# Block 1's q in an attention + SwiGLU kernel: half of its transfers issued by ScalarE, its two turns placed around block 0's last product of h, and block 0's sums behind them

## The chip, the core and the metric

The kernel runs on one core of a Trainium2 chip. TensorE (PE; its weight loads are shown apart as PEld) multiplies, VectorE (DVE), ScalarE (ACT) and GpSimd (POOL) work on tiles, SyncE (SP) only issues DMAs, and ACT can issue them too. Each engine runs its own instruction list strictly in order and meets the others through semaphores. The metric is the device time of one launch in microseconds (us), as the median of several runs.

## What is computed

Inputs are float32. Attention is linear (no softmax): for each of 8 batches and 8 heads a 64x64 matrix is made from k and v, q is multiplied by it, and each row of 64 is divided by its root mean square. The result, laid out as 4608 tokens by 512, goes through a SwiGLU block with 1536 hidden columns.

```
kv  = einsum('bhsd,bhse->bhde', k, v)          # 8 batches, 8 heads, 576 positions, 64 wide
o   = einsum('bhsd,bhde->bhse', q, kv)
o   = o / sqrt(mean(o * o, -1) + 1e-6) * g_norm
x   = o.transpose(0, 2, 1, 3).reshape(4608, 512)
g, val = x @ w_gate, x @ w_val                 # 512 x 1536 each
out = (g * sigmoid(g) * val) @ w_out           # 1536 x 512
```

## The kernel before

The 4608 tokens are nine blocks of 512. For each block an `Att` object makes x (attention, turned so that features lie on partitions) and an `Ffn` object makes h = silu(x w_gate) * (x w_val) and then h w_out. Blocks 0, 1 and 2 run alone, the other six in pairs. Most of the feed-forward multiplications use Strassen's scheme in Winograd's form: seven products (numbered 1 to 7) take the place of eight, and VectorE and GpSimd make the sums and differences of operands and results that it needs. The time of interest is the end of block 0 and the start of block 1, some 98 to 160 us into the launch.

**Block 0, up.** Block 0's h is made without Strassen, in `plain_up(f)` for f = 0 to 11: eight matmuls into one `b` and one `c` bank of PSUM (L1475), ScalarE's silu of `b` into h (L1480), VectorE's product of h with `c` (the helper `mul`, L133). Beside it the weights are loaded by SP (L177) and rounded by VectorE and ScalarE (L188 to L204); the last of them go into `wo`. Then `t2` takes a difference and a sum in `wo` (helpers `sub`, L132, and `add`, L131).

**Block 1's inputs.** When the last weight pieces are under way, SP issues block 1's k and v (L317, 288 KB each) and its q (L338): two halves of 16 small DMAs each, 8 of 56 KB and 8 of 8 KB, all with runs of 32 floats, into two tiles of the pool `ld`. `turn_q(0)` and `turn_q(1)` transpose the two halves on VectorE (L391) into one tile `qt`. A half of q here is a half of the heads, so each of block 1's products `heads` (L436) needs both.

**Block 0, down.** `plain_end` makes the sums of h: s1 = a21 + a22 (L131, 128x1536) and, over a21 in place, s1 - a11 (L132, 128x1536). Then `Ffn.down` issues the seven products of the down multiplication (`Quad.multiply`, L663) in the order 1, 6, 5, 7, 2, 4, 3 as traced, into the banks `b` (1, 6, 7, 4), `c` (5, 3) and `a` (2). Product 1 takes a11 alone, product 6 the new a21, product 5 takes s1. Each product is 24 matmul records. What follows them:

- after product 1, block 1's `heads` for both halves (L436), then on ScalarE their squares (L449), on VectorE four row sums (L450), an inverse root by nine 128x32 steps (L466 to L481), four scalings (L133) and two transposes (L515), then 16 DMAs (L527, 8 from SP and 8 from ACT) that put the turned blocks into x, ScalarE's gain (L534) and four sums of x on VectorE;
- `turn_s3`: one more difference in h (L132, 128x1536);
- after product 2 (`after2`): r = a + s (L131), then s4, a difference in h that product 3 multiplies (L132, 128x1536);
- after product 7 (`after7`): ScalarE copies `b` (L1376), and VectorE adds `c`, which holds product 5, to that copy (L131). Product 3 goes on into the same `c`, so it cannot start before this add has read the bank;
- `t2` on the six tiles `wv[j]` (for each a `sub` and an `add` of 128x512): j = 0 to 2 behind block 1's scaling, j = 3 to 5 behind s4. Block 1's weights need them, GpSimd's own differences `t` (L132 on POOL) among them.

**kept_steps.** Six steps for each half of a pair of weight tiles: three differences and a sum on VectorE (128x256 to 128x512), and two DMAs that send them to DRAM (L1259). They are handed to `ffn.later` in `Up.multiply` and taken by `make`.

**What sets the order.** The language traces instructions and a scheduler at compile time decides the order in which each engine gets them, by dependencies and by its own estimate of times. `tc.issue_after(i)` says that what is traced inside it and runs on i's engine comes behind i on that engine; it makes no wait between engines. `in_order` keeps the traced order on the engines named. So an edit can move instructions that its lines do not name.

Of the kernel before, what the change touches and what calls it, by code (L numbers as in the profile page):

```python
# [8 lines left out]
F32 = mybir.dt.float32  # L9
# [3 lines left out]
ACT = mybir.ActivationFunctionType  # L13

P = 128
# [3 lines left out]
def kernel(  # L19
# [41 lines left out]
    nc = tc.nc  # L61

    B, H, S, D = q.shape
    NT, DM = out.shape
    FF = moe_w_gate.shape[1]
    T = 4
    BLK = P * T
    HB = BLK // 2
    HD = DM // 2
    NB = NT // BLK  # L70
    NS = DM // P
    NF = FF // P
    NP = NF // 2
# [12 lines left out]
    s_pool = pool("s", 1)  # L86
# [148 lines left out]
    class Att:  # L235
# [305 lines left out]
        def sum_steps(self):  # L541

            a11, a12, a21, _, s1, s3, s4 = (self.x[:, i] for i in range(7))
            yield lambda: add(nc.vector, s1, a21, self.x[:, 3])
            yield lambda: sub(nc.vector, s3, a21, a11)
            yield lambda: sub(nc.vector, a21, s1, a11)
            yield lambda: sub(nc.vector, s4, a12, a21)
# [137 lines left out]
    class Up(Quad):  # L685
# [29 lines left out]
        def after7(self):  # L715
            self.u3 = self.piece(2)
            copied = nc.scalar.copy(out=self.u3, in_=self.ps["b"])

            if self.j < NP - 1:
                with tc.issue_after(copied.ins):  # L720
                    nc.scalar.activation(out=self.s, in_=self.s, func=ACT.Silu)
            added = add(nc.vector, self.u3, self.ps["c"], self.u3)

            owed, self.ffn.owed = self.ffn.owed, None
            if owed:
                with tc.issue_after(added.ins):
                    owed()
# [18 lines left out]
        def multiply(self, p):  # L746
            super().multiply(p)
            ffn = self.ffn
            if ffn.n == 1:
                if p == 5:  # L750
                    self.leaf_room = chunks(ring())
                if p in (5, 7, 4):
                    at = 3 * (5, 7, 4).index(p)
                    ffn.making.extend(leaf_steps(self.j, [(self.w[p].unsqueeze(1), (p,))], self.leaf_room[:, at:]))
                if p == 3:
                    if self.j < 2:
                        ffn.later.extend(kept_steps(self.j, chunks(xi_alone)))

    class Inner:

# [531 lines left out]
    def chunks(t):  # L1292

        return t.rearrange("p f (s c) -> p (f s) c", c=P) if len(t.shape) == 3 else t.rearrange("p a b c -> p (a b) c")

    def kept_steps(j, room):


        for i, (t, os) in enumerate(kept(j)):
            b11, b12, b22 = t[:, :, 0, 0], t[:, :, 0, 1], t[:, :, 1, 1]  # L1300
            to = room[:, 8 * i : 8 * (i + 1)].rearrange("p (o r) c -> p o r c", r=4)
            t2_ = to[:, :, 0]
            yield lambda b22=b22, b12=b12, t2_=t2_: sub(nc.vector, t2_, b22, b12)
            yield lambda b11=b11, t2_=t2_: add(nc.vector, t2_, t2_, b11)
            yield lambda t=t, t2_=t2_, to=to: sub(
                nc.vector, to[:, :, 2:4], t[:, :, 1], t2_.unsqueeze(2).to_broadcast([P, 2, 2, P])
            )
            yield lambda t2_=t2_, os=os: send_leaf(j, os, (6,), t2_)
            yield lambda b11=b11, t2_=t2_, to=to: sub(nc.vector, to[:, :, 1], b11, t2_)
            yield lambda to=to, os=os: send_leaf(  # L1310
                j, os, (7, 4, 5), to[:, :, 1:4].rearrange("p o r c -> p o (r c)")
            )
        if j < 2:
            yield from raw_steps(j)
# [72 lines left out]
    class Ffn:  # L1387
        def __init__(self, n, att):
            self.n, self.att = n, att
            self.h = h_alone if n < PAIRED else h_slots[(n - PAIRED) % 2]  # L1390
            self.ps, self.ended, self.owed = {}, None, None

            self.making, self.later = [], []
            self.chores, self.sends = [], []
            self.visited = None
# [5 lines left out]
        def h_sums(self, j, k, engine):  # L1401

            h = self.h.rearrange("p (j e) t -> p j e t", e=2)[:, j : j + k]
            a11, a21, a22 = h[:, :, 0, 0:HB], h[:, :, 0, HB:BLK], h[:, :, 1, HB:BLK]
            s1 = self.s1[:, j : j + k]
            add(engine, s1, a21, a22)
            return sub(engine, a21, s1, a11)

        def make(self, count):
            for _ in range(count):  # L1410
# [55 lines left out]
        def plain_up(self, f, halves=(0, 1)):  # L1466

            if 0 in halves:
                self.ps[f] = [pool.tile([P, 2, HB], F32, name=pool.name[0]) for pool in (b_psum, c_psum)]
            of = slice(halves[0], halves[-1] + 1)  # L1470
            ps = [t[:, of] for t in self.ps[f]]
            x = self.att.x[:, 0:4].rearrange("p (h m) i t -> p (m i) h t", h=2)
            for t, w in zip(ps, (wg, wv)):
                for i in range(NS):
                    nc.tensor.matmul(  # L1475
                        t, lhsT=w[f // 2][:, i, P * (f % 2) : P * (f % 2 + 1)], rhs=x[:, i, of],
                        start=(i == 0), stop=(i == NS - 1),
                    )
            h = self.h[:, f].rearrange("p (h t) -> p h t", h=2)[:, of]
            nc.scalar.activation(out=h, in_=ps[0], func=ACT.Silu)  # L1480
            mul(nc.vector, h, h, ps[1])

        def plain_end(self):

            self.s1 = s_pool.tile([P, NP, HB], F32, name="s1")
            self.h_sums(0, NP, nc.vector)
            self.down_ = Down(self)
            self.down_.turn_t(5)

# [72 lines left out]
    def t2(place, b22, b11):  # L1562

        sub(nc.vector, place, b22, place)
        add(nc.vector, place, place, b11)

    blocks = [Att(n) for n in range(NB)]
    blocks[0].room = h_alone
# [55 lines left out]
    def alone(n):  # L1624
        ffn = Ffn(n, blocks[n])
        nxt = blocks[n + 1]
        if n == 0:

            with tc.issue_after(squared.ins), tc.issue_after(scaled.ins):
                weights(2)  # L1630
            ffn.plain_up(0, (0,))
            copied = blocks[0].copied
            blocks[0].turn_x(1)
            for f in range(NF):
                with tc.issue_after(blocks[0].copied.ins if f else copied.ins):
                    weights(2 * (f + 2))
                ffn.plain_up(f) if f else ffn.plain_up(0, (1,))
            weights(len(pieces))
            pairs = wo.rearrange("p (j e) d -> p e j d", e=2)
            t2(pairs[:, 0, :, HD:DM], pairs[:, 1, :, HD:DM], pairs[:, 0, :, 0:HD])  # L1640
            nxt.room = xi_alone.rearrange("p a b c -> p (a b c)")

            with tc.issue_after(sent.ins):
                for i in range(2):
                    nxt.load_kv(i)
                for i in range(2):
                    nxt.load_q(i)
            ffn.plain_end()
            for g in range(2):
                nxt.kv(g)  # L1650
            nxt.turn()
        elif n == 1:

            def third():
                visit(ffn, nxt, (0, 1))
                for i in range(2):
                    nxt.load_q(i)

            ffn.up({(1, 7): third})
            nxt.turn()  # L1660
            blocks[PAIRED].load_kv(0)
        else:
            with in_order(nc.vector.engine, nc.scalar.engine):
                ffn.up(ahead(ffn, nxt, blocks[PAIRED + 1]))
            nxt = blocks[PAIRED + 1]
            nxt.turn()
            for g in range(2):
                blocks[PAIRED + 2].load_kv(g)
        if n == 2:
            ffn.down_.opens = PAIRED  # L1670

        def inner_sums():
            with tc.issue_after(nxt.scaled.ins):
                blocks[PAIRED].inner_sums()

        def second_kv():
            with tc.issue_after(nxt.placed.ins):
                blocks[PAIRED].load_kv(1)

        ffn.down(nxt, {1: {5: second_kv}, 2: {7: inner_sums}}.get(n, {}))  # L1680
        if n == 0:
            for g in range(2):
                blocks[2].load_kv(g)

            with tc.issue_after(nxt.halves[0].ins):
                for j in range(NP // 2):
                    t2(wv[j][:, 0:2], wv[j][:, 2:4], wg[j][:, 0:2])
            with tc.issue_after(ffn.down_.s4.ins):
                for j in range(NP // 2, NP):
                    t2(wv[j][:, 0:2], wv[j][:, 2:4], wg[j][:, 0:2])  # L1690

    for n in range(PAIRED):
        with in_order(nc.tensor.engine) if n == 2 else ExitStack():
            alone(n)
# [65 lines left out]
```

## Time and profile before

| What | Value |
|---|---|
| median of 3 runs | 1005.79 us (1004.57 to 1006.64) |
| the profiled execution's own time | 1004.97 us |
| its span from first to last instruction | 1003.2 us |
| granted TensorE clock over the span | 1.0 |
| instructions | 17762 |
| idle of PE over the span, 1003.2 - 986.9 | 16.3 us |
| HBM traffic | 109.12 MB read, 32.83 MB written |

A timeline row of the profile gives the start in us from the span's start, the time to the last end, the engine, the line, the operation, out<-in with the number of partitions and elements, and how many instructions were merged; in brackets stands the idle time before them and what ended it. An engine name with a q (SPq, ACTq, DVEq) is that engine's queue, which issues DMAs and waits. In the lists of waits a row says who waited for whom, with the sum, the number of times and the longest in us. Two of the steps above in numbers: SP's 32 issues of q took from 98.98 to 118.50 us, and the DMA engines were busy 0.40 of the time between 104.0 and 113.8 us, when only q was moving.

### The profile page before, as it was taken

How to read it: one execution, taken by the hardware profiler on the slowest of the kernel's cores; microseconds unless marked ns; L12 is line 12 of the kernel's file. 1: busy time of each engine (PE TensorE's matmuls, PEld its weight loads, DVE VectorE, ACT ScalarE, POOL GpSimd, SP SyncE). 2: the span in 40 equal slices, each digit the busy share in tenths (PEclk: the TensorE clock that was granted, in tenths of full speed). 3: DMA queues.
4: the chain of work that ended last, by engine and by line, in shares of the span. 5: the costliest groups of instructions: out<-in, count | busy, mean ns of one | idle time of the engine just before them, and what ended most of it. 6: DMA issues, size and time to landing. Idle time of an engine off the chain costs nothing.

```text
span 1003.2 us, 17762 instructions
## 1 busy us (share of the span) xinstructions
PE 986.9 (98%) x6758; PEld 833.6 (83%) x6758; DVE 713.1 (71%) x1171; ACT 231.5 (23%) x367; POOL 408.1 (41%) x328
## 2 busy tenths in 40 slices
PE   5999999999999999999999999999999999999998
PEld 4544688888888888888888888888888888888998
DVE  2999797579958576656675846666776576666894
ACT  2765111221122312121211211122112112222100
POOL 0000263255544240444566003555651078999300
PEclk9999999999999999999999999999999999999999
DMA  8689643473866855666752365667312556565123
GB/s 228 199 261 268 123 87 137 102 271 107 210 135 132 205 114 167 178 193 168 171 151 43 97 158 151 158 180 177 112 18 68 118 169 204 182 213 161 48 83 97
DMA packets 268261, 151.54 MB, mean 151 GB/s; under 512 B 150288, under 2 KB 250128, under 8 KB 268176
## 3 DMA queue, kind: packets, MB, share of 16 engines
q1 hardware_dynamic: 235280, 145.41, 53.4%
q10 hardware_dynamic: 32832, 4.99, 2.8%
q8 instruction: 54, 0.88, 0.4%
q14 instruction: 31, 0.25, 0.1%
q0 software_dynamic: 64, 0.00, 0.0%
HBM read 109.12 MB, written 32.83 MB: 142 GB/s over the span
## 4 chain that ended last, share of the span: by engine, by line
PE 76%; DVE 0%; DVEq 0%; issue 0%
PE b L818 22%; PE b L663 16%; PE c L818 11%; PE c L663 8%; PE a L818 5%; PE a L663 4%; PE b L897 4%; PE c L897 2%; PE m L436 1%; PE a L897 1%; PE m L375 1%; PE b L375 0%; PE b L436 0%; PE a L436 0%; PE a L375 0%; DVE r L131 0%
## 5 line engine op out<-in xcount | busy, mean ns | idle before, releaser
L818 PE MATMUL b<-arena,t 128*128 128x256 f32 x1008 | 244.5, 381 | 0.0
L818 PEld LDWEIGHTS b<-arena,t 128*128 128x128 f32 x1008 | 190.0, 190 | 29.6 <-DVE r L131 2.4
L131 DVE TENSOR_TENSOR r<-b,r 128x512 f32<-128x512 f32 (+1 forms) x248 | 146.1, 601 | 67.3 <-PE b L818 54.8
L131 POOL TENSOR_TENSOR r<-r 128x256 f32<-128x256 f32 (+1 forms) x90 | 94.6, 1053 | 168.3 <-DMA t<-w 93.3
L131 DVE TENSOR_TENSOR r<-c,r 128x512 f32<-128x512 f32 (+1 forms) x171 | 105.6, 625 | 59.8 <-PE c L818 39.9
L133 POOL TENSOR_TENSOR arena<-r 128x1024 f32<-128x1024 f32 (+1 forms) x54 | 102.1, 1905 | 94.8 <-DVE r L131 48.8
L131 DVE TENSOR_TENSOR r<-a,r 128x512 f32<-128x512 f32 x95 | 60.3, 635 | 100.1 <-PE a L663 65.9
L132 POOL TENSOR_TENSOR t<-wo 128x512 f32<-128x512 f32 x45 | 64.1, 1447 | 162.6 <-DVE wo L131 105.2
L132 DVE TENSOR_TENSOR arena<-arena 128x512 f32<-128x512 f32 (+4 forms) x117 | 122.3, 1063 | 9.2 <-PE b L663 6.9
L818 PE MATMUL c<-arena,t 128*128 128x256 f32 x504 | 122.5, 379 | 0.0
L818 PEld LDWEIGHTS c<-arena,t 128*128 128x128 f32 x504 | 95.5, 190 | 13.4 <-issue 0.2
L663 PE MATMUL b<-wo,arena 128*128 128x256 f32 x336 | 76.8, 382 | 0.2
L832 ACT COPY r<-b 128x512 f32<-128x512 f32 x54 | 31.7, 586 | 189.8 <-PE b L818 189.8
L663 PE MATMUL b<-t,arena 128*128 128x256 f32 x336 | 74.8, 379 | 0.0
L132 POOL TENSOR_TENSOR t<-arena 128x512 f32<-128x512 f32 x36 | 51.1, 1433 | 54.0 <-PE c L663 21.3
L663 PEld LDWEIGHTS b<-wo,arena 128*128 128x128 f32 x336 | 62.9, 190 | 10.0 <-DVE arena L133 0.9
L663 PEld LDWEIGHTS b<-t,arena 128*128 128x128 f32 x336 | 63.8, 190 | 8.7
L818 PE MATMUL a<-arena,t 128*128 128x256 f32 x252 | 66.1, 379 | 0.0
L818 PEld LDWEIGHTS a<-arena,t 128*128 128x128 f32 x252 | 47.9, 190 | 6.5
L663 PE MATMUL b<-arena 128*128 128x256 f32 x192 | 45.5, 380 | 0.0
L663 PE MATMUL b<-arena,t 128*128 128x256 f32 x192 | 45.4, 379 | 0.0
L1475 PE MATMUL b<-arena 128*128 128x512 f32 (+1 forms) x104 | 43.5, 561 | 0.5 <-ACT arena L500 0.5
(142 smaller groups left out, 1407.6 us busy)
## 6 DMA issues: line engine op xcount, KB each, us to landing
t<-w SPq DMA_DIRECT2D x180, 256.0 KB, 3.3
ld<-in_k_dram SPq DMA_DIRECT2D x26, 288.0 KB, 4.6
ld<-in_v_dram SPq DMA_DIRECT2D x26, 288.0 KB, 5.8
out_dram<-r SPq DMA_DIRECT2D x14, 512.0 KB, 3.3
t<-w SPq DMA_DIRECT2D x54, 128.0 KB, 2.5
ld<-in_moe_w_gate_dram SPq DMA_DIRECT2D x12, 512.0 KB, 4.9
ld<-in_moe_w_val_dram SPq DMA_DIRECT2D x12, 512.0 KB, 4.7
ld<-in_moe_w_out_dram SPq DMA_DIRECT2D x12, 512.0 KB, 5.0
```

Of the source, the lines that this page charges most:

```text
L131: add = lambda e, o, a, b: e.tensor_tensor(out=o, in0=a, in1=b, op=OP.add)
L132: sub = lambda e, o, a, b: e.tensor_tensor(out=o, in0=a, in1=b, op=OP.subtract)
L133: mul = lambda e, o, a, b: e.tensor_tensor(out=o, in0=a, in1=b, op=OP.mult)
L375: self.positions = nc.tensor.matmul(self.kv_ps[r][u * D : (u + 1) * D, g, :], lhsT=k[:, u, c, :], rhs=v[:, u, c, :], start=(c == 0), stop= ...
L436: self.multiplied = nc.tensor.matmul(self.ps[i][u][p : p + D, t, j, :], lhsT=self.qt[rows, tile_t, head, p : p + D], rhs=kvs[b % 3][rows, ...
L663: self.ffn.multiplied = nc.tensor.matmul(ps[:, e], lhsT=lhsT, rhs=rhs, start=first and i == 0 and e == 0, stop=i == self.steps - 1, skip_g ...
L818: self.ffn.multiplied = nc.tensor.matmul(ps[:, i], lhsT=stream.use(self.ffn.n, self.j, o, p), rhs=self.operand(o, p), start=first and i == ...
L832: copied = nc.scalar.copy(out=dst, in_=ps)
L897: self.ffn.multiplied = nc.tensor.matmul(ps[:, i, f], lhsT=self.deep.operand(o, p, c)[:, f], rhs=self.deep.weight(o, p, c, f), start=first ...
L1475: nc.tensor.matmul(t, lhsT=w[f // 2][:, i, P * (f % 2) : P * (f % 2 + 1)], rhs=x[:, i, of], start=(i == 0), stop=(i == NS - 1),)
```

## The change

In block 0's branch of `alone`, q's first half stays on SP; the 16 DMAs of the second half are issued by ScalarE, behind the silu of f = 10. `turn_q(0)` is ordered on VectorE behind `t2` of `wo`, the product of h for f = 11 behind `turn_q(0)`, and `turn_q(1)` behind that product. s1 is made in a list of its own behind `turn_q(1)`, in written order: s1, then six steps of block 0's `kept_steps` (the first half of pair 0), then the difference over a21. In block 1's `Up` the remaining steps of `kept_steps(0)` come behind block 1's last scaling, and those of `kept_steps(1)` behind the add after product 7 of pair 0.

```
-            for f in range(NF):
+            for f in range(NF - 1):
                 with tc.issue_after(blocks[0].copied.ins if f else copied.ins):
                     weights(2 * (f + 2))
                 ffn.plain_up(f) if f else ffn.plain_up(0, (1,))
...
-            t2(pairs[:, 0, :, HD:DM], pairs[:, 1, :, HD:DM], pairs[:, 0, :, 0:HD])
+            turned = t2(pairs[:, 0, :, HD:DM], pairs[:, 1, :, HD:DM], pairs[:, 0, :, 0:HD])
...
             with tc.issue_after(sent.ins):
                 for i in range(2):
                     nxt.load_kv(i)
-                for i in range(2):
-                    nxt.load_q(i)
+                nxt.load_quarters(0)
+            with tc.issue_after(ffn.silus[NF - 2].ins):
+                for step in nxt.quarter_steps(1, (0, 1), (nc.scalar,)):
+                    step()
+            with tc.issue_after(turned.ins):
+                nxt.turn_q(0)
+            with tc.issue_after(nxt.q_turned.ins):
+                multiplied = ffn.plain_up(NF - 1)
+            with tc.issue_after(multiplied.ins):
+                nxt.turn_q(1)
+            ffn.s1 = s_pool.tile([P, NP, HB], F32, name="s1")
             ffn.plain_end()
             for g in range(2):
                 nxt.kv(g)
-            nxt.turn()
+            with in_order(nc.vector.engine), tc.issue_after(nxt.q_turned.ins):
+                one, two = ffn.sum_steps()
+                one()
+                for _ in range(6):
+                    first_kept.pop(0)()
+                two()
...
+    first_kept = list(kept_steps(0, chunks(xi_alone)))
```

```
+        def sum_steps(self):
+
+            h = self.h.rearrange("p (j e) t -> p e j t", e=2)
+            a11, a21, a22 = h[:, 0, :, 0:HB], h[:, 0, :, HB:BLK], h[:, 1, :, HB:BLK]
+            return lambda: add(nc.vector, self.s1, a21, a22), lambda: sub(nc.vector, a21, self.s1, a11)
...
         def plain_end(self):
 
-            self.s1 = s_pool.tile([P, NP, HB], F32, name="s1")
-            self.h_sums(0, NP, nc.vector)
             self.down_ = Down(self)
             self.down_.turn_t(5)
...
+            if self.j == 0:
+                self.ffn.added = added
...
                     if self.j < 2:
-                        ffn.later.extend(kept_steps(self.j, chunks(xi_alone)))
+                        first, *steps = first_kept if self.j == 0 else kept_steps(self.j, chunks(xi_alone))
+
+                        def held():
+                            with tc.issue_after((ffn.added if self.j else ffn.att.scaled).ins):
+                                first()
+
+                        ffn.later += [held, *steps]
```

More of the change, by code (lines that the diff above doesn't have):

```diff
@@ L1390, in __init__ @@
             self.h = h_alone if n < PAIRED else h_slots[(n - PAIRED) % 2]
-            self.ps, self.ended, self.owed = {}, None, None
+            self.ps, self.silus, self.ended, self.owed = {}, {}, None, None
             self.making, self.later = [], []
@@ L1479, in plain_up @@
             h = self.h[:, f].rearrange("p (h t) -> p h t", h=2)[:, of]
-            nc.scalar.activation(out=h, in_=ps[0], func=ACT.Silu)
-            mul(nc.vector, h, h, ps[1])
+            self.silus[f] = nc.scalar.activation(out=h, in_=ps[0], func=ACT.Silu)
+            return mul(nc.vector, h, h, ps[1])
         def plain_end(self):
-            self.s1 = s_pool.tile([P, NP, HB], F32, name="s1")
-            self.h_sums(0, NP, nc.vector)
             self.down_ = Down(self)
@@ L1564, in t2 @@
         sub(nc.vector, place, b22, place)
-        add(nc.vector, place, place, b11)
+        return add(nc.vector, place, place, b11)
     blocks = [Att(n) for n in range(NB)]
```

## The prediction

> **What bounds the kernel now.** First the page: what is busy, and what ended last.
>
> ```profile
> PE   5999999999999999999999999999999999999998
> ...
> PE 76%; DVE 0%; DVEq 0%; issue 0%
> ```
>
> The chain that ended last is TensorE's (PE's) own work; once loading is over no other engine is on it. So an edit pays what idle time it takes from PE and costs what it adds there. The whole list of PE's waits, its first start-up rows left out:
>
> ```profile
> PE m L436 <- DVE r L391: 0.8, 2, 0.5
> PE b L1475 <- ACT arena L500: 0.5, 2, 0.3
> ...
> PE m L499 <- DVE r L133: 0.3, 1, 0.3
> PE c L663 <- DVE r L131: 0.2, 1, 0.2
> ```
>
> The rows of L1475 and L499 belong to block 0's beginning. What is left lies at 121 us (0.8, block 1's `heads` for the turns of q, which the change is at) and at 150 us (0.2, product 3 for `after7`'s add). So the change can win 0.8 + 0.2 = 1.0 us, 0.10% of the time; a measurement here tells no less than about 0.2% (2.0 us) from no change. The two places in PE's timeline:
>
> ```profile
> 121.78 0.24 PE L436 MATMUL m<-kv,r 64*64 64x64 f32 x1 [0.46 <-DVE r L391]
> ...
> 122.81 0.27 PE L436 MATMUL m<-kv,r 64*64 64x64 f32 x1 [0.34 <-DVE r L391]
> ...
> 145.19 5.34 PE L663 MATMUL b<-t,arena 128*128 128x256 f32 x24
> 150.76 5.45 PE L663 MATMUL c<-wo,arena 128*128 128x256 f32 x24 [0.23 <-DVE r L131]
> 156.04 1.89 PE L663 MATMUL b<-arena 128*128 128x256 f32 x8
> ```
>
> VectorE (DVE) in the same stretch:
>
> ```profile
> 113.78 0.69 DVE L133 TENSOR_TENSOR arena<-arena,c 128x512 f32<-128x512 f32 x1 [5.21 <-PE c L1475]
> 114.50 2.58 DVE L131 TENSOR_TENSOR s<-arena 128x1536 f32<-128x1536 f32 x1
> ...
> 120.39 2.36 DVE L391 STREAM_TRANSPOSE r<-ld 128x1024 f32<-128x1024 f32 x2
> 122.68 1.72 DVE L132 TENSOR_TENSOR arena<-arena 128x1536 f32<-128x1536 f32 x1
> ...
> 147.16 0.68 DVE L131 TENSOR_TENSOR r<-a,r 128x512 f32<-128x512 f32 x1
> 147.76 2.34 DVE L132 TENSOR_TENSOR arena<-arena 128x1536 f32<-128x1536 f32 x1
> 150.03 0.68 DVE L131 TENSOR_TENSOR r<-c,r 128x512 f32<-128x512 f32 x1
> 150.63 2.83 DVE L132 TENSOR_TENSOR arena<-arena 128x512 f32<-128x512 f32 x2
> ```
>
> To be seen: from 113.78 to beyond 158 VectorE is late. Product 2 ended at 145.35 (start 140.01 + 5.34), yet its add (147.16) waits in a row without an idle time in brackets; so does the add into which product 3 must not run (150.03 to 150.71; PE starts at 150.76). Behind it come two `sub` of `t2`, 2.83 us for both, while GpSimd works (POOL is busy 3.31 of the 3.80 us from 147.2 to 151.0). A `sub` of that shape without such company takes 0.60 us from start to start (the rows from 154.59 on).
>
> **The order that the build gives.** I read both programs' orders engine by engine. On VectorE, up to the add of `after2`, it is what the diff says, with one more move: `turn_s3` (L132 at 122.68) now follows the four row sums. Then, after s4, the order is `sub`, `sub`, and only then `after7`'s add; before it was that add, then the two `sub`. The diff names none of these. On PE, `heads` take half 0 first, then half 1, and one matmul of product 5 stands before product 6. GpSimd's order is unchanged, and past block 1's up VectorE's is too.
>
> **1. The transfers.** SP issued 32; the first eight waited for older loads (starts 98.98 to 105.29), the rest came every 0.5 us to 118.07, and landing took 2.0 us (median), so q was whole at 120.0. Now SP and ScalarE issue 16 each, but each waits, at every issue, for the one four before it, where SP alone waited for the eighth. SP gets four away until 105.3, then three rounds of four, each lasting as long as a landing L: the last issue is at 105.5 + 2L + 1.5 and lands at 107.0 + 3L. ScalarE starts behind the silu of f = 10 (103.41 + 0.60) and is at most half a microsecond behind. L is not shown for two queues of q; the bounds are 2.0 (one queue) and the 2.7 that is the least of L527's 16 transfers from both queues (2.7, 3.6, 4.1 least, median, most), each with 512 runs against q's 448 and 64 by turns. I take 2.45, between the two and nearer to L527's least, since two queues will be at work but the DMA engines were busy only 0.40 of the time under one (104.0 to 113.8 us); for the range 2.0 to 3.0. Both halves are there at 114.35 (113.0 to 116.0).
>
> [...]
>
> **2. Turns and h.** `turn_q(0)` 1.17, product of h 0.60, `turn_q(1)` 1.15 and 0.1 of waits follow: E, the end of `turn_q(1)`, is 110.0 + 3L = 117.35 (116.0 to 119.0). The silu of f = 11 moves behind ScalarE's 16 issues, from 110.27 to some 112.4; it is ready before the product of h at 115.5. That product is 1.7 us later than now; product 1 doesn't use f = 11, and its other h was ready at 108.5. Next in ScalarE's list stand the copies of block 1's kv (115.96 before), which `heads` want at 121.3; behind SP's half come block 2's k and v (wanted at 176.86) with two sends of `kept` steps among them, which wait for VectorE until some 121.5 and hold nothing up: SP's next work is the placing of x at 134. `heads` find q turned at 121.32, where product 1 ends: -0.46 - 0.34 = -0.80 us on PE.
>
> **3. The sums, now behind the turns.** s1 2.50, four `kept` steps 1.65, the difference 1.70 (starts 114.50, 117.00, 117.33, 119.00 and 119.45 to 120.39): the new a21 is ready at E + 5.85 = 123.2. Product 6 would start at 121.32 + 2.25 (`heads`) + 0.43 = 124.0, so 0.8 us cover it; with E = 119.0 it would wait 0.85. Row sums 2.45 and `turn_s3` 1.75 end at E + 10.05 = 127.4; the root began at 126.97 before. So VectorE's chain is D = E - 116.9 = 0.45 us later. It cannot be early by more than the squares allow (after `heads` they end at some 124.7, a row sum and `turn_s3` behind that): D is 0.1 to 2.1. ScalarE's gain and the sums of x move by D as well and have room: the gain ended at 146.2, x is wanted at 156.
>
> **4. The add before product 3.** From the root to s4 VectorE has no pause (12.96 of 13.00 us busy from 134.2 to 147.2), and GpSimd's differences wait for VectorE's `t2`, so all of it shifts by D. After s4 come the two `sub` first: 2.75 us (150.63 to 153.38), as GpSimd's third difference still runs beside them; 1.20 if it did not; 3.35 if both met it all the way (the slower one took 1.67). The add starts at 150.03 + 0.45 + 2.75 = 153.23 and PE 0.73 later at 153.96, against 150.76: **+3.20 us**. The 0.80 us of step 2 are swallowed here, since PE only comes to this wait earlier (149.7). Bounds: 0.1 + 1.20 = +1.3, and 2.1 + 3.35 = +5.45.
>
> [...]
>
> **5. Behind it.** Product 3 runs to 159.2 and block 1's up begins there, not at 156.04. The two `add`, the `sub`, the `add` and the four sums of x end at 153.9 + 8 x 0.6 = 158.7, so x is not late. PE has no further wait in the list that could take the shift back. The kept steps in block 1 change places among VectorE pauses (2.61, 1.57, 0.99 us) and cost nothing while these last; were one gone, 1.6 us would fall on an add whose bank PE wants ten microseconds later.
>
> Sum: 1004.97 + 3.20 = 1008.2 for an execution like the profiled one, which lies 0.8 below the median shown; set on the median, 1005.79 + 3.2 = **1009.0 us**.
>
> **Rivals.** *A, the forecast*: product 3 waits for the add behind two `sub`; own range 1007.1 to 1011.2; chance 0.71. *B, the add is early all the same*: PE keeps 0.80 + 0.23, 1005.79 - 1.0 = 1004.8. It decides if VectorE ends the add before 149.7, 4.2 us earlier than worked out. For it: the ten operations from 134.18 to 147.16 would take only some 5.2 us without GpSimd's company, so a small drift apart could give that back. Against: GpSimd's first difference is released by VectorE (137.56, after an idle of 1.33), so it drifts along. Chance 0.13. *C, two queues as slow as L527's median*, L = 3.6: E = 120.8, D = 3.9, +3.9 + 2.75 = 1012.4. For it: the only row with both queues; against: half the runs for each transfer. Chance 0.11. *D, the change does not bring q earlier*: ScalarE needs 0.91 for each issue (L527's 7.28 for 8), 14.6 from 104.0, and 2.0 to land: E = 121.8, D = 4.9, +7.65 = 1013.4, and `heads` wait on. Against: q's small transfers take SP 0.48, not 0.80. Chance 0.05.
>
> **From these the numbers.** Range 1005.3 to 1012.2: A's whole, the upper half of B and the lower of C. Slower by over 0.2%: A without its low corner (0.64), C and D: 0.79. Within 0.2%: B and that corner, 0.19. Faster by over 0.2%: more than all of PE's idle time that the change can reach, so only scatter of the runs, 0.02.
>
> **What would show it.** Right: no wait of `heads` on L391; PE idle some 4 us before product 3, ended by DVE L131; on VectorE s4, two `sub` of 128x512, then the add of `c`; all later stages some 3 us later. Step 1 is wrong if q's median landing is above 3.0, step 3 if product 6 waits. The forecast falls if GpSimd is idle while the six `t2` run, or if the add ends before 150.

## The result: 1011.18 us, and the profile after

The changed kernel takes 1011.18 us (median of 5 runs, 1010.13 to 1012.62), the kernel before 1006.09 us beside it (5 runs, 1004.57 to 1006.64). The ratio is 1.0053, 95% interval 1.0041 to 1.0064: slower by 0.5%, about 5.1 us. The profiled execution took 1012.62 us with a span of 1010.8 us, 7.6 us above the 1003.2 of before.

The recorded mean granted clock of the five runs is 0.996, 0.997, 0.998, 0.998 and 0.997 (the first is the profiled one); the runs of the kernel before that have it on record read 1.0 or 0.999.

First the top of the list of PE's waits in the changed kernel (us in total, times, longest):

```profile
PE b L299 <- DMA arena<-in_v_dram: 5.8, 2, 5.2
PE c L663 <- DVE r L131: 4.7, 1, 4.7
PE b L397 <- DMA ld<-in_q_dram: 4.1, 1, 4.1
```

The wait of `heads` for L391, 0.8 us before, is no longer in it. Product 3's wait for `after7`'s add has grown from 0.2 to 4.7 us. The first row belongs to the start of the launch, where the wait for loads differs from profile to profile (5.8 us here, 5.1 in the kernel before): PE reached block 0's down 1.25 us later than in the profile of before (117.12 against 115.87), and that much is taken off below wherever a time is called aligned. Product 1 in the kernel before:

```profile
115.87 5.45 PE L663 MATMUL b<-wo,arena 128*128 128x256 f32 x24
```

PE's timeline of the changed kernel:

```profile
117.12 5.45 PE L663 MATMUL b<-wo,arena 128*128 128x256 f32 x24
124.52 0.70 PE L663 MATMUL c<-t,s 128*128 128x256 f32 x2
125.05 1.24 PE L663 MATMUL b<-wo,arena 128*128 128x256 f32 x5
...
155.41 7.97 PE L663 MATMUL c<-wo,arena 128*128 128x256 f32 x24 [4.73 <-DVE r L131]
163.22 1.89 PE L663 MATMUL b<-arena 128*128 128x256 f32 x8
```

Product 3 starts at 155.41, aligned 154.16, 3.40 us later than before. And it takes 7.97 us with the same 24 records that took 5.45. VectorE's timeline shows why it starts late:

```profile
116.20 1.25 DVE L391 STREAM_TRANSPOSE r<-ld 128x1024 f32<-128x1024 f32 x1 [6.30 <-DMA ld<-in_q_dram]
117.37 0.65 DVE L133 TENSOR_TENSOR arena<-arena,c 128x512 f32<-128x512 f32 x1
117.94 1.23 DVE L391 STREAM_TRANSPOSE r<-ld 128x1024 f32<-128x1024 f32 x1
119.09 1.72 DVE L131 TENSOR_TENSOR s<-arena 128x1536 f32<-128x1536 f32 x1
...
122.58 1.75 DVE L132 TENSOR_TENSOR arena<-s,arena 128x1536 f32<-128x1536 f32 x1
...
148.60 0.68 DVE L131 TENSOR_TENSOR r<-a,r 128x512 f32<-128x512 f32 x1
149.20 5.56 DVE L132 TENSOR_TENSOR arena<-arena 128x1536 f32<-128x1536 f32 x3
154.68 0.68 DVE L131 TENSOR_TENSOR r<-c,r 128x512 f32<-128x512 f32 x1
```

The row of 5.56 us holds s4 and the two `sub` of `t2`; only then comes the add that reads `c`. Why product 3 is then slow is seen in a table of stretches (length, busy time of PE, PEld, DVE, ACT and POOL with counts, then the granted clock and the DMA engines):

```profile
146.91:150.32 3.41, 3.41 (x18) 2.99 (x16) 3.41 (x4) 0.60 (x1) 3.41 (x3) 1.00 0.00 0
150.32:153.73 3.41, 0.37 (x2) 0.00 (x0) 3.41 (x3) 0.59 (x1) 3.41 (x2) 1.00 0.00 0
153.73:157.14 3.41, 1.73 (x4) 1.47 (x5) 3.41 (x5) 0.00 (x0) 0.48 (x1) 0.50 0.24 92
157.14:160.56 3.41, 3.41 (x9) 2.71 (x9) 3.30 (x6) 0.00 (x0) 0.00 (x0) 0.50 0.17 62
160.56:163.97 3.41, 3.41 (x17) 3.00 (x17) 0.55 (x1) 0.00 (x0) 0.00 (x0) 1.00 0.02 5
```

The first number behind the comma in each row is PE's busy time. PE fell idle at 150.69; from 153.73 to 160.56 the granted clock is 0.50. In the last half-rate stretch PE, busy all the time, began 9 matmuls; in the full-rate one, 17. So the wait cost PE not only the time that it stood still but 2.5 us of slow work behind it (7.97 - 5.45).

Of the profiled 7.6 us, 1.25 are the start, 3.40 the later start of product 3, 2.5 its slow part, and some 0.4 are left for the 850 us behind. There PE's list has two waits that the kernel before does not have: 0.7 us at 318 us for a load of v (L375) and 0.2 us for a weight (L826).

Not every run need have lost as much as the profiled one. The half-rate stretch in the table is 6.83 us long, two times the 3.41 us that one lasts in e8 and e11 below; an estimate from these lengths: each 3.41 us at half rate takes 1.7 of some 1009 us, 0.0017, off the mean clock. So two of the five runs (0.998) fit one such stretch, the other three fit two.

### The profile page after: what moved, and what is told of

It reads as the page before. It is cut to its first block, busy times and chain, and to the rows that moved or that the text cites. A ratio compares the mean times of both kernels' runs of the same rounds, so it can differ in the third digit from the quotient of the medians.

```text
span 1010.8 us, 17762 instructions
## 1 busy us (share of the span) xinstructions
PE 989.5 (98%) x6758; PEld 835.8 (83%) x6758; DVE 715.4 (71%) x1171; ACT 231.4 (23%) x367; POOL 408.5 (40%) x328
## 4 chain that ended last, share of the span: by engine, by line
PE 90%; DVE 4%; DMA 3%; ACT 1%; issue 0%; SPq 0%; POOL 0%; ACTq 0%; DVEq 0%; POOLq 0%
PE b L826 22%; PE b L663 20%; PE c L663 11%; PE c L826 11%; PE a L826 5%; PE a L663 5%; PE b L905 4%; PE b L1489 4%; PE c L1489 3%; DVE arena L132 2%; PE c L905 2%; PE m L436 1%; PE m L375 1%; DMA ld<-in_q_dram 1%; DMA arena<-in_v_dram 1%; PE a L905 1%
## 5 line engine op out<-in xcount | busy, mean ns | idle before, releaser
L826 PE MATMUL b<-arena,t 128*128 128x256 f32 x1008 | 244.4, 381 | 0.0
L826 PEld LDWEIGHTS b<-arena,t 128*128 128x128 f32 x1008 | 190.0, 190 | 29.3 <-DVE r L131 2.1
L826 PE MATMUL c<-arena,t 128*128 128x256 f32 x504 | 122.5, 379 | 0.2 <-DMA t<-w 0.2
L826 PEld LDWEIGHTS c<-arena,t 128*128 128x128 f32 x504 | 95.5, 190 | 13.8 <-DVE r L131 0.5
L826 PE MATMUL a<-arena,t 128*128 128x256 f32 x252 | 66.1, 379 | 0.0
L826 PEld LDWEIGHTS a<-arena,t 128*128 128x128 f32 x252 | 47.9, 190 | 6.5
L663 PE MATMUL c<-wo,arena 128*128 128x256 f32 x168 | 40.0, 398 | 4.7 <-DVE r L131 4.7
```

The lines of the kernel that those rows point to most:

```text
L663: self.ffn.multiplied = nc.tensor.matmul(ps[:, e], lhsT=lhsT, rhs=rhs, start=first and i == 0 and e == 0, stop=i == self.steps - 1, skip_g ...
L826: self.ffn.multiplied = nc.tensor.matmul(ps[:, i], lhsT=stream.use(self.ffn.n, self.j, o, p), rhs=self.operand(o, p), start=first and i == ...
```

## The experiments

All were timed beside the kernel before on the same chip. Its medians were 1006.30 us (30 runs) for e1 to e4, 1005.86 us (21 runs) for e5 to e8 and 1005.88 us (22 runs) for e9 to e12. Three dots in an edit stand for lines left out.

**e1: is it the place of the add?** The changed kernel, with `after7`'s add ordered ahead of the last three `t2`.

```
-            add(nc.vector, self.o2[:, :, HD:DM], self.ps["c"], u3)
+            self.added = add(nc.vector, self.o2[:, :, HD:DM], self.ps["c"], u3)
...
-            with tc.issue_after(ffn.down_.s4.ins):
+            with tc.issue_after(ffn.down_.s4.ins), tc.issue_after(ffn.down_.added.ins):
                 for j in range(NP // 2, NP):
```

> The changed kernel, but t2 of j = 3 to 5 comes behind after7's add, so VectorE's order after s4 is add, sub, sub as before the change. Theory (the order of that add is the whole loss): in the changed kernel's profile VectorE reached after2's add 0.2 us later than before, once the later start is taken off, so product 3 starts 0.2 to 0.5 us later than before, PE idles some 1.4 us there and the granted clock stays at 1.0 through product 3 (5.3 us long, not 8.0). Time 1006.1 + 0.2 to 0.6, that is 1006.3 to 1006.7. Rival (the split of the transfers or the moved kept steps cost something elsewhere): it stays above 1008. Rival (the half clock in product 3 has a cause other than the idle time before it): product 3 still takes 8 us, 1009.

Measured: 1005.88 us, ratio 0.9995 (0.9986 to 1.0004). The whole loss is gone; the time is 0.4 us under the lowest expected. Product 3 in e1's PE timeline:

```profile
150.88 5.45 PE L663 MATMUL c<-wo,arena 128*128 128x256 f32 x24 [1.39 <-DVE r L131]
```

It waits 1.39 us and runs at full rate. The rest of the change costs nothing that these runs can tell, but it wins nothing either: what `heads` gave PE is spent in this wait.

**e2: wait or clock?** The changed kernel, with nine matmuls that nobody needs between products 4 and 3, into a bank that nobody reads. The add stays late; PE is kept busy until shortly before it.

```
+                if self.n == 0 and p == 4:
+                    spare = m_psum.tile([P, 2, HB], F32, name="m")
+                    with tc.issue_after(self.multiplied.ins):
+                        for _ in range(9):
+                            filler = nc.tensor.matmul(spare[:, 0], lhsT=ident, rhs=wo[:, 0, 0:HD], start=True, stop=True)
+                    self.filler = filler
...
```

The lines left out order product 3 behind the last of the nine. In the profile the nine are 18 records.

> The changed kernel with 9 matmuls (128x256, result not used) between products 4 and 3, 3.9 us of work in the 4.7 us in which PE idled. Theory (the clock halves because PE idles over 3 us): the add still comes when it came, product 3 starts when it started but runs in 5.3 us at clock 1.0; time 1011.2 - 2.5 = 1008.7. Rival (the half clock comes with VectorE's and GpSimd's work or with the wait itself): product 3 still takes 8 us and the time is 1011.

Measured: 1008.94 us, ratio 1.0024 (1.0014 to 1.0034). e2's PE timeline:

```profile
148.91 4.05 PE L1471 MATMUL m<-wo,ident 128*128 128x256 f32 x18
153.80 5.45 PE L663 MATMUL c<-wo,arena 128*128 128x256 f32 x24 [0.85 <-DVE r L131]
```

PE's idle time is 0.85 us, product 3 is back at 5.45, and useless work has made the kernel faster. The late add alone costs 1008.94 - 1006.30 = 2.6 us; the halved clock is the rest of the 5.1, some 2.5. (In e2's profile product 3 starts 3.41 us later than before, once the start is aligned; why the medians show 2.6 of that is not settled.)

**e3: the order alone.** The kernel before, with nothing changed but that two `sub` of `t2` stand ahead of `after7`'s add.

```
-                    t2(wv[j][:, 0:2], wv[j][:, 2:4], wg[j][:, 0:2])
+                    first = sub(nc.vector, wv[j][:, 0:2], wv[j][:, 2:4], wv[j][:, 0:2])
+                    if j < NP - 1:
+                        tc.add_manual_dep(
+                            ffn.down_.added.ins, first.ins.name,
+                            mybir.DependencyInfo(mybir.DependencyClass.NoSync, mybir.DependencyReason.DATA),
+                            reason="order",
+                        )
+                    add(nc.vector, wv[j][:, 0:2], wv[j][:, 0:2], wg[j][:, 0:2])
```

> The kernel before with one thing of the change: the first two subs of t2 for j = 3 and 4 stand ahead of after7's add on VectorE. Theory: product 3 starts 2.75 us later (153.5 us), after 3.0 us of idle time; without a drop of the clock 1006.1 + 2.8 = 1008.9, with one up to 1011.4 (the drop came some 3.0 us after PE fell idle, so this stands on the edge). Rival (the loss needs the moved turns or the second queue): 1006.

Measured: 1010.32 us, ratio 1.0043 (1.0027 to 1.0058). e3's PE timeline:

```profile
154.57 7.13 PE L663 MATMUL c<-wo,arena 128*128 128x256 f32 x24 [3.57 <-DVE r L131]
```

Two VectorE operations in another order, with q untouched, cost 4.0 of the 5.1 us. The profile is that of the slowest of the seven runs (1014.65 us) and holds more than the edit. Its clock halved a second time, from 318.49 to 321.90: PE had waited there 1.0 and 0.7 us for loads of v (L375) and was busy only 1.72 of the 3.41 us ahead of the fall. The median run has no profile. Its mean clock is 0.999, as is that of the run of 1009.12 us, which fits no half-rate stretch; three runs have 0.998 and the other 0.996. So the order alone is enough for the late add; the clock fell with it in some runs and, by this sign, not in all.

**e4: what would the change bring if the add were early?** e1, with the second half of block 0's `kept_steps` behind `after7`'s add as well (they stood between the root and s4; `marks["added"]` is that add).

```
-                            with tc.issue_after((ffn.added if self.j else ffn.att.scaled).ins):
+                            with tc.issue_after((ffn.added if self.j else marks["added"]).ins):
...
```

> As the first of these, and the second half of kept_steps(0) (four VectorE steps, 5.9 us in the changed kernel beside GpSimd) waits behind after7's add. Theory (VectorE's lateness between 134 and 150 us is what PE waits for): VectorE reaches after2's add before PE ends product 2, PE has no wait at heads nor at product 3, 1006.1 - 1.0 = 1005.1. Rival (the kept steps only move to where PE waits for the sums of x or for GpSimd's differences): above 1006.

Measured: 1004.47 us, ratio 0.9978 (0.9970 to 0.9987), faster than both kernels. VectorE in e4:

```profile
144.11 0.69 DVE L131 TENSOR_TENSOR r<-a,r 128x512 f32<-128x512 f32 x1 [2.80 <-PE a L663]
144.72 1.79 DVE L132 TENSOR_TENSOR arena<-arena 128x1536 f32<-128x1536 f32 x1
146.43 0.68 DVE L131 TENSOR_TENSOR r<-c,r 128x512 f32<-128x512 f32 x1
```

VectorE now waits for PE (2.80 us) where PE waited for VectorE, and the add is done at 147.1. PE's timeline of e4 has product 3 directly behind product 4, without brackets:

```profile
143.91 5.34 PE L663 MATMUL b<-t,arena 128*128 128x256 f32 x24
149.09 5.34 PE L663 MATMUL c<-wo,arena 128*128 128x256 f32 x24
```

**e5: is the second queue needed?** The changed kernel, with q's second half back in SP's queue.

```
-            with tc.issue_after(ffn.silus[NF - 2].ins):
-                for step in nxt.quarter_steps(1, (0, 1), (nc.scalar,)):
-                    step()
+            with tc.issue_after(sent.ins):
+                nxt.load_quarters(1)
```

> The changed kernel with the second half of block 1's q back in SyncE's queue, behind the first; VectorE's order is the changed one. If the second queue is what brings q early, the second half lands at about 120.0 as before the change, turn_q(1) ends at about 121.3 instead of 117.9, the sums behind it and with them after7's add come some 3.3 us later, product 3 waits 8 us instead of 4.7, and the time is 1014.4 (1013 to 1016.5). [...]

Measured: 1014.96 us, ratio 1.0090 (1.0077 to 1.0103). The second half is turned from 119.14 on, after VectorE has waited 4.60 us for it. In e5's list of PE's waits the delay has split in two:

```profile
PE c L663 <- DVE r L131: 5.1, 1, 5.1
...
PE b L663 <- DVE arena L132: 1.6, 1, 1.6
```

The second row is product 6, waiting for the new a21 (step 3's cover of 0.8 us used up). The time came out as expected, the split not: all 8 us had been expected at product 3.

**e6: the second queue alone.** The kernel before, with only the second half of q issued by ScalarE behind the silu of f = 10.

```
-                for i in range(2):
-                    nxt.load_q(i)
+                nxt.load_quarters(0)
+            with tc.issue_after(ffn.silu.ins):
+                for step in nxt.quarter_steps(1, (0, 1), (nc.scalar,)):
+                    step()
...
```

> The kernel before with one part of the change alone: the second half of q is issued by ScalarE behind the silu of f = 10; VectorE's order is that of the kernel before. In it the turns of q started at 120.39 with no idle time of VectorE before them, behind the sums of h. If VectorE's order was the limit of heads and the transfers were hidden behind it, the time is that of the kernel before, 1006.1 +- 0.5, and heads still wait some 0.3 to 0.8 us for L391. If the late landing of q at 120.0 was the limit, heads find q turned, PE keeps up to 0.8 us there, and the time is 1005.3 or, where product 3's add swallows it, 1006.1 without a wait of heads.

Measured: 1005.87 us, ratio 1.0002 (0.9993 to 1.0011), no change. `heads` still wait 1.0 us for L391. SP's last issue of q is 6 us earlier (112.1 against 118.1), but in VectorE's list the turns stand behind the sums, with no idle time in front of them:

```profile
115.12 2.52 DVE L131 TENSOR_TENSOR s<-arena 128x1536 f32<-128x1536 f32 x1
...
120.97 2.36 DVE L391 STREAM_TRANSPOSE r<-ld 128x1024 f32<-128x1024 f32 x2
```

So neither half of the change works without the other: the queue alone is hidden behind VectorE's order, the order alone makes VectorE wait for q.

**e7: the two moves of e4 without q.** The kernel before, with the add ahead of the last three `t2` and the second half of `kept_steps(0)` behind it.

```
+                        steps = list(kept_steps(self.j, chunks(xi_alone)))
+                        if self.j == 0:
+                            seventh = steps[6]
+
+                            def held():
+                                with tc.issue_after(marks["added"].ins):
+                                    seventh()
+
+                            steps[6] = held
+                        ffn.later.extend(steps)
...
-            with tc.issue_after(ffn.down_.s4.ins):
+            with tc.issue_after(ffn.down_.s4.ins), tc.issue_after(ffn.down_.added.ins):
...
```

> The kernel before, q and its turns as they were, with the two moves that made the changed kernel faster than both: after7's add ahead of the two sub of t2, and the second half of the first kept steps behind that add. If these moves only set free what q's change had won (0.8 to 1.1 us at heads), little is won here: product 3's own wait of 0.2 us goes, heads keep theirs, and the time is 1005.9 (1005.3 to 1006.4). If the moves win by themselves, whatever q does, the time is 1004.5 as it was with q's change (1004.47).

Measured: 1005.32 us, ratio 0.9993 (0.9984 to 1.0002): as expected in size. But one reason fell: `heads` did not wait in its profile. That is taken up with e10.

**e8: how long an idle time costs the clock?** e2 with four matmuls in place of nine.

> The changed kernel with 4 instead of 9 unused matmuls between products 4 and 3 (their result goes nowhere), so that PE's idle time before product 3 is about 2.9 us instead of 4.7 (none) or 0.85 (nine). If the clock halves only behind an idle time of about 3 us and more, it stays at full rate here, product 3 takes 5.45 us, and the time is that with nine, 1008.9 +- 0.5. If a shorter idle time is enough, product 3 takes 7 to 8 us and the time is 1010.5 to 1011.5.

Measured: 1010.96 us, ratio 1.0053 (1.0039 to 1.0066). The first of the two values expected fell: 2.99 us of idle time cost the clock too, and all five runs have a mean clock of 0.998. Its stretches, cut at the changes of the clock:

```profile
153.00:156.41 3.41, 0.98 (x5) 0.88 (x6) 3.41 (x5) 0.00 (x0) 1.23 (x1) 1.00 0.02 6
156.41:159.82 3.41, 3.41 (x10) 2.66 (x9) 3.35 (x6) 0.00 (x0) 0.00 (x0) 0.50 0.41 152
159.82:163.24 3.41, 3.41 (x17) 3.02 (x16) 1.34 (x3) 0.00 (x0) 0.00 (x0) 1.00 0.00 0
```

PE was already back at work at 155.43 when the clock fell at 156.41. The 3.41 us ahead of the fall had 0.98 us of work in them, so PE had not been idle all through.

**e9 and e10: e4's kernel and e7's once more, on one chip.** No edit is new.

> The kernel of e4_kept_later once more, beside the same two moves without the change of q, on one chip. If q's earlier landing and turns are worth the 0.8 us that heads waited for, it is 1004.5 +- 0.4 and some 0.8 us below the other; if the two moves alone make the gain, both are at one time.

> The kernel of e7_before_kept_later once more, beside the one with q's change. Its heads found q turned in the profiled execution, because GpSimd's six differences had begun 1.3 us earlier than in the kernel before and the sum of h had run without them (1.76 us instead of 2.58). If that holds in most executions, it ties with e9; if heads mostly wait, it is some 0.8 us above e9, at 1005.3 +- 0.4.

Measured: 1003.93 us, ratio 0.9983 (0.9974 to 0.9992), with q's change, and 1005.90 us, ratio 0.9999 (0.9990 to 1.0008), without. So once the add is early, the rest of the change (q's transfers and turns, and the new places of `kept_steps`) does earn something, 1.97 us between the medians here, more than the 0.8 expected; the two intervals leave room for some 0.3 to 2.9 us. Between e7 and e4, on two chips, it was 1.3 us, each median taken less that of the kernel before beside it. In the profile of e10, as in e7's, `heads` find q turned. VectorE in e10:

```profile
114.65 1.79 DVE L131 TENSOR_TENSOR s<-arena 128x1536 f32<-128x1536 f32 x1
...
119.75 2.36 DVE L391 STREAM_TRANSPOSE r<-ld 128x1024 f32<-128x1024 f32 x2
```

s1 takes 1.79 us, against 2.58 in the kernel before, because in this execution GpSimd's six differences of `wo` were nearly over. GpSimd in e10, and then in the kernel before:

```profile
107.43 7.38 POOL L132 TENSOR_TENSOR t<-wo 128x512 f32<-128x512 f32 x6 [104.58 <-DVE wo L131]
```

```profile
108.06 7.40 POOL L132 TENSOR_TENSOR t<-wo 128x512 f32<-128x512 f32 x6 [105.21 <-DVE wo L131]
```

They begin when VectorE's `t2` of `wo` ends, and that differs from profile to profile: 8.59 us ahead of product 1 in e10 (8.92 in e7), 7.81 in the kernel before and 7.87 in e6, where `heads` waited. Up to this point VectorE, ScalarE and GpSimd have the same operations in the same order in the kernel before, e7 and e10, so this is not their edit. In the kernel before, ScalarE's rounding (L188) still waited for a weight of `w_out` until 99.43; in e10 its last such wait ended at 96.42. So the wait of 0.8 us that the change was at is there in some executions and not in others. e10's profiled execution (1003.8 us) is among its fastest, e9's (1005.6 us) is its slowest; the eleven times lie from 1003.0 to 1007.6 and from 1003.1 to 1005.6. A wait of 0.8 us in part of the executions would make less than the 1.97 us between the medians; what else differs in e10's slower ones was in no profile and stays open.

**e11 and e12: e2 with five and with seven matmuls.**

> The changed kernel with 5 unused matmuls between products 4 and 3, an idle time of PE of about 2.55 us in front of product 3. With 4 of them (2.99 us) the time was 1010.96, with 9 (0.85 us) 1008.94. If the clock's limit lies between 2.55 and 2.99, the time is 1008.9 +- 0.4; if it lies below, 1010.5 to 1011.3.

> The same with 7 unused matmuls, an idle time of about 1.7 us. If the clock is kept at some idle time between 1.7 and 2.99 us, this one has it, 1008.9 +- 0.4, and product 3 takes 5.45 us; if even 1.7 us is too much (1.39 us kept it in e1_add_first), 1010.5 to 1011.3.

Measured: e11 1009.35 us, ratio 1.0035 (1.0023 to 1.0048), one run at 1011.07 and four from 1008.1 to 1009.4; e12 1008.82 us, ratio 1.0031 (1.0019 to 1.0044). e11's profile is of the run at 1011.07; its stretches:

```profile
151.12:154.53 3.41, 0.85 (x4) 0.39 (x3) 3.41 (x4) 0.00 (x0) 2.22 (x2) 1.00 0.00 0
154.53:157.95 3.41, 3.41 (x8) 2.78 (x9) 3.38 (x6) 0.00 (x0) 0.00 (x0) 0.50 0.41 154
```

And product 3 in e12's PE timeline:

```profile
155.13 5.45 PE L663 MATMUL c<-wo,arena 128*128 128x256 f32 x24 [1.70 <-DVE r L131]
```

An idle time of 1.70 us kept the clock in the profile, and all six runs of e12 have a mean clock of 1.0, the slowest (1010.83 us) too, whose time is not explained. One of 2.57 us lost it in e11's profiled run. Of e11's five runs two have a mean clock of 0.998 (1011.07 and 1009.35 us), two 1.0 (1008.10 and 1008.24) and one 0.999 (1009.36): it seems to have been lost in some runs and kept in others. The mean clock is only a hint; one run each of e7 and e10, whose profiles have no wait of PE here, reads 0.998 as well. So e11's expectation, a limit on one side or the other of 2.55, was put too simply.

## Why the prediction was right, and where its sum was short

The mechanism was right: `heads`' wait went, product 3 waited for the add behind two `sub`, and all that stood behind it moved. The sum was 2.2 us short (1009.0 against 1011.18), by about the size of one missing term, the halved clock. That the result lies inside the range is partly luck: rival A's own range reached 1011.2 by adding a chain that is 2.1 us late to two `sub` that meet GpSimd all the way, and the chain was only 0.2 us late; its upper end held nothing for the clock.

- **Step 1, the transfers.** With L = 2.45 both halves were to be whole at 114.35. The first turn began at 116.20, where its wait for q ended, aligned 114.95: 0.6 us later. Landing took 2.3 us (median, on both queues), less than the 2.45 taken, so it was not L that was too small: the issues came later than worked out. SP's last started at 113.6 and ScalarE's at 114.3, aligned 112.4 and 113.1, where 111.9 had been worked out. That the two queues would be needed was right: in e5 the one queue's last issue of q was at 115.8 us, VectorE waited for the second half until 119.14, and the time was 1014.96 us. The DMA engines had room under one queue and under two: they were busy 0.40 of the time in the kernel before (104.0 to 113.8 us) and 0.65 in the changed one (104.0 to 114.3). So issuing and waiting for landings was the limit here. Rival C (L = 3.6) and rival D fall with the same row.
- **Step 2, the turns and h.** `turn_q(1)` ended at 119.09, aligned 117.84, against 117.35. After `heads` PE went on to its next work 1.1 us earlier (124.52, aligned 123.27, against 124.37 before), where 0.8 us had been predicted.
- **Step 3, the sums.** s1 was priced at 2.50 us from the row of before; it took 1.72, since at 119.09 GpSimd's differences were over (they ended at 116.80). Its own rows could have told: in the kernel before they ended at 115.46, ahead of the 117.35 worked out for s1. That paid for the later landing: the new a21 was there at 124.33, aligned 123.08, against 123.2, and product 6 had no wait. VectorE came to s4 only 0.2 us late, where 0.45 had been worked out.
- **Step 4, the add.** The two `sub` took 5.48 - 2.27 = 3.2 us from start to start (s4 taken as in the kernel before), against 2.75. With D 0.25 smaller and the `sub` 0.45 dearer the add came 3.40 us later instead of 3.20. The 0.80 us of `heads` were swallowed as said. e1 shows that the place of the add is enough to undo the loss, e3 that it makes most of it by itself.
- **What failed in step 4 and step 5.** Product 3 "starts 153.96" was worked out, and then "runs to 159.2", that is for 5.3 us: the step priced the wait as lost time only and took the matmuls behind it at full rate. The granted clock halved, product 3 took 7.97 us, and +3.20 became +5.9 in the profile (3.40 + 2.5). e2 separates the two: the same late add without the idle time costs 2.6 us of the 5.1. In the profile of before the granted clock reads 1.0 all through, and no idle time of four microseconds lies in the stretch that was studied. At the launch's start `ident` matmuls of 128x128 (L397) take 0.43 us each between 4 and 8 us, behind a wait of 4.1 us, and 0.29 us each behind 18 us; the clock reads 1.0 at both, so that the wait made them slow was not shown. No price of the clock was worked out before the run.
- **Step 5, behind it.** That nothing takes the shift back held: some 0.4 us were left over 850 us. The waits of 0.7 us (L375) and 0.2 us (L826) that appeared there were not foreseen; e7, with q as before, has both as well (0.5 and 0.2), so they are not put down to the change.
- **Rival B** asked for an add that ends before 149.7 and gave 1004.8 us. That is the kernel of e4: its add is done at 147.1 and it takes 1004.47 us. But B's reason, a drift of VectorE and GpSimd apart, did not come about: the ten operations ahead of `after2`'s add took 13.0 us in the changed kernel (135.60 to 148.60), as before. Nor are the two `sub` all that stood in the way: in e1, with the add ahead of them, it still ended only at 150.83. It took the later `kept_steps` of e4 as well. Why the scheduler put the two `sub` ahead was not tested.

## What to carry to other kernels

A microsecond won on the engine that sets the pace is only kept if the next thing that this engine waits for comes earlier as well: follow the freed engine to its next wait before you price a gain. Read the order that the build gives, not only the lines of the edit, and look for operations that slipped in front of the one somebody waits for. Where a change lets TensorE stand still for as long as it did here when the clock halved (2.57 to 5.11 us before product 3, and once 1.7 in two pieces), look for half-rate work behind the wait and price it: product 3 took 7.11 to 8.21 us then, in place of 5.45. Reordering (e1, 1005.88 us), or even useless matmuls (e2, 1008.94 us), was cheaper than the wait (1011.18 us).

## What the runs showed of the hardware

- The half-rate stretches between product 3 and the end of a launch last 3.41 us or twice that: 6.83 in the changed kernel and in e5, 3.41 in e8, in e11 and twice in e3.
- PE need not be idle all through for the clock to fall. In the 3.41 us ahead of a fall it had 0.37 (changed kernel), 0.98 (e8) and 0.85 us (e11) of work; in the changed kernel the clock stayed half behind 3.41 us with 1.73 us of work, and came back behind 3.41 us filled with work. An idle time of 2.57 us was enough once (e11), 1.70 us (e12) and 1.39 us (e1) did not halve it. But 1.70 us is not safe: in e3 two waits with 1.69 us in the 3.41 us ahead of the second fall were enough, 1.72 us of work in them. Near the end of the kernel before, 3.41 us with 1.50 us of work (997.73 to 1001.14) had a clock of 1.0 behind them, so the busy time as the profile counts it gives no single limit. Why an idle time of some 2.5 us halved the clock in some of e11's runs and, by their mean clock, not in others was not shown.
- The price follows from the busy time at half rate: in e8 3.41 / 2 = 1.7 us, and product 3 took 7.13 - 5.45 = 1.7 us longer; in the changed kernel 155.41 to 160.56, 5.15 / 2 = 2.6, against 2.5.
- The same operation of VectorE (s1) took 1.72 to 2.58 us, by whether GpSimd was at work beside it. How long GpSimd's work still ran beside it went, in the profiles compared under e10, with when a weight had landed (ScalarE's last wait for one ended at 99.43 us in the kernel before and at 96.42 in e10). A wait of 0.8 us in one profile was therefore not there in every one.
